# Norm scans and attention angles in the attention's two PSUM banks, with all operations in a new order

## The chip, the cores and the metric

One core of one Trainium2 chip runs the kernel. The time is the device time of one execution in microseconds (us); lower is better. Six engines matter: TensorE (PE, with its weight loads as PEld), VectorE (DVE), ScalarE (ACT), GpSimd (POOL), and SyncE (SP), which issues most DMAs.

## The reference

An attention with a decaying complex state is followed, per token, by a feed-forward network (FFN) with a rational activation. Four batches, eight heads, 768 steps, head width 48; the FFN is 384 to 2048 to 384.

```python
mag = sqrt(a_re**2 + a_im**2)
scale = minimum(mag, 0.999) / (mag + 1e-6)
a_re_n, a_im_n = a_re * scale, a_im * scale
for t in range(S):
    ar, ai = a_re_n[:, :, t, :, None], a_im_n[:, :, t, :, None]
    new_re = ar * S_re - ai * S_im
    new_im = ar * S_im + ai * S_re
    S_re, S_im = new_re + outer(k[t], v[t]), new_im
    y[t] = q[t] @ S_re
x = y.transpose(0, 2, 1, 3).reshape(B * S, H * D)
h = x @ w_in
P = a[0] + a[1]*h + a[2]*h**2 + a[3]*h**3
Q = 1.0 + abs(b[0])*abs(h) + abs(b[1])*h**2
out = (P / (Q + 1e-6)) @ w_out
```

## The kernel before

The 768 steps are cut into 6 chunks of 128; a chunk of one batch is a *unit*, so there are 24 units, taken in 12 pairs. For a unit the decay is turned into magnitude and angle from the chunk's start, so that a chunk becomes ordinary attention plus a carried state.

- `norm` (L498) squares a_re and a_im, gets magnitudes, and runs three scans of 128 columns (L524) that multiply the magnitudes up along the chunk. The second factor of the scans, 1 - 2 EPS x, is written to SBUF over `SQ` (L518) by ACT, DVE or POOL.
- `angle` (L528) works on a pair: ACT's Arctan over `T` (768 columns, L557), one scan over the 768 columns that sums the angles (L539), a maximum for a range test (L540), whole turns as integers in `CO` (the `turn`, L543), their subtraction (L545), and the carry `thc`. Two sines follow (`trig`, L550).
- `outer` (L569) multiplies q and k (`QK`) with magnitudes (`RU`) and then with cosines and sines (`Q`, two halves), and sends them with six DMAs a unit to one of two tiles `HQ`, where heads lie side by side.
- `attn` (L597) does the matmuls of a unit: transposes (L611), evacuated to `kT`; scores (L624), masked to `ST`; values (L642), copied to `X`; state update (L662), added to `St`. Each of these takes one of two PSUM banks (`at`, L337), in turn, in the order in which the code creates them.
- `ffn` (L678) works through the 16 blocks of 128 hidden columns: matmuls into `ph` (L701), eight elementwise instructions on ACT and DVE (one of them, the low product `g`, on POOL or DVE), matmuls into `po` (L717). The first two pairs use full-width float32 weights, later pairs weights split in a high and a low part (`halve`, L461).
- `weights` (L454) reads the weights, which are double precision, in 28 loads and folds them into float32 on ACT, DVE and POOL. `rouse` (L665) adds dummy matmuls in the start.

No engine order follows from the code's order: every operation goes into a `Plan`, and a table (`ORDER`) read by `recorded` gives the order in which operations are issued, and for those that may run on several engines also the engine. Each engine runs its own instructions in that order, and waits by semaphores. In the plan, an operation that uses a PSUM operand is not counted on the port that DVE and POOL share (`port=not psum`, L360).

Of the kernel before, what the change touches and what calls it, by code (L numbers as in the profile page):

```python
# [227 lines left out]
def act(n, psum=False):  # L228
# [11 lines left out]
    "xW?Gfe`CcMEjQAOwT#bRyO5qm=!=T3l;6riEXS*%A9dsSPxdfcOJnmdn<BT#T1GXd{uPU(nzWQAW`R|*2Kn+cZVw%d`8@f*R}toCvcz<<%aoxFrX5werA11z"  # L240
    "a+ND)<d;fF_Tz@obU!1PvFFMuGLLa9kW~U)iVv4bXrNAH)^dsWD%Td>AY+M(kuFW{#SU8VE1ikgR!YKhJ~N|O$;J3oJ}cxkMh~;oq?sJTbg4>P5xEa_B#mP)"
    "W=`OKUzJDdzkO^y{=-;&jhjux%!rP|Khag5lnQ!30l+^PgZZ>IMF#3AwuV}v+v(}iJ@~hza`jT&i%qCWixrrGF?{w@J>?d<4X7>;nPk_CvEE5P71viBUxq@Q"
    "B=QREYVNgjPVVur6zY*KUC!V|J(u@abg3OhYgKqfI3txPPsFn~YRZhjQW=I~sr18H+%5;{`)XN@okZIh943-?Vt2ijQ6<Y|U;G0`Wil<L%AXjuKiSJzB6HA7"
    "R%s>Axl6?A2l0<(0%J3Umg5+UjrF7Gd~9R=?Xh;pmmp;Nx<Z^lk}Q-usz-dfjKWm$e$7QZ=TK1-&iV!qU@t4TuXyw%nRB)Y>trhZtiW@)L-OQhaD07LG#2~x"
    "9yb>QWU<aGt|P<a*U4GpZzSIXh4ghCF2Km7`h$;UnlWw^Hpo%j!1Z3xvt2&o7%b1o3VM@euA<l`oBDFh4#pw_46x)2`Ku|lRRlUks>svK@OnHg)0wxK(x2bI"
    ")s5Xl^nISL=`QFoc9cnxnl4G25KCt{`)}wb#~8!jSjk`C>e+UZ8SD-d0}(09JR>7q8LqNMx9E<}=V3Y8bI0f8CfW@1D(AbuqIZD$mvnaVFjSz22}!!k(GR#C"
    "dLn0ij8t>LUd46NtFlfyasTDmrH{y4tfO&yl6ze<uI>m<lG{$oOI-a5*=`{#IhEP{9=DSHK9ZS?!w51+4Aaa``!MUZg|6c6;h2}@3*2Q6;1TQNdPHt!6clSs"
# [865 lines left out]
```

## Time and profile before

| | |
|---|---|
| median of 3 runs | 608.46 us (607.23 to 609.35) |
| the profiled execution | 608.84 us |
| its span in the trace | 607.1 us |
| TensorE busy | 558.8 us, 92% |
| DVE busy | 545.7 us, 90% |
| ACT busy | 527.1 us, 87% |
| POOL busy | 275.4 us, 45% |

"Busy" is the sum of an engine's instructions; weight loads run beside matmuls and are counted apart. A page of the profile gives these sums, the timeline lists single instructions in order of time with the idle time before them and its releaser in brackets, and the table of stretches gives busy time by engine for parts of the span. `PEclk` is the granted TensorE clock as a share of 2.4 GHz; 0.5 is the lower level, 1.2 GHz.

### The profile page before, as it was taken

Reading aid. Unit: us, or ns where it says so; the run is one execution under the profiler, and the core shown is the slowest. Engines: PE = TensorE matmul, PEld = TensorE weight load, DVE = VectorE, ACT = ScalarE, POOL = GpSimd, SP = SyncE. Lnnn points to the kernel's source line nnn. Section 1 sums busy time; section 2 is a strip of 40 time slices with the busy share of each in tenths; the row PEclk is TensorE's granted clock in tenths of the full one; section 3 lists DMA queues with packets and bytes.
Section 4 is the critical chain, followed back from the end, with each engine's and each line's share of the span. In section 5 each row is a group of like instructions: output and inputs, shape, how many; then the busy total and the mean of one; then the engine's idle time right before and its main releaser. Section 6 shows DMA issues by size and latency. Waiting matters only on the chain.

```text
span 607.1 us, 15647 instructions
## 1 busy us (share of the span) xinstructions
PE 558.8 (92%) x6236; PEld 468.3 (77%) x6236; DVE 545.7 (90%) x918; ACT 527.1 (87%) x870; POOL 275.4 (45%) x264
## 2 busy tenths in 40 slices
PE   3258989999999999998999999999999999999995
PEld 2246878778899999996888877888888888778884
DVE  6989979989999999999999999988899978779983
ACT  6978989989999999999999989988978787587871
POOL 4456455255655556624684544464726066200000
PEclk9669999999999999999999999999999999999998
DMA  8899436436551455537227147233464235010001
GB/s 268 282 253 285 148 79 152 111 57 149 110 136 41 89 128 127 129 103 154 51 64 157 35 106 168 74 60 82 75 102 127 26 73 103 3 52 2 1 1 58
DMA packets 39185, 64.02 MB, mean 105 GB/s; under 512 B 4416, under 2 KB 25152, under 8 KB 39104
## 3 DMA queue, kind: packets, MB, share of 16 engines
q1 hardware_dynamic: 38960, 62.67, 42.2%
q8 instruction: 51, 0.84, 0.6%
q14 instruction: 30, 0.25, 0.1%
q10 hardware_dynamic: 144, 0.26, 0.1%
HBM read 39.32 MB, written 4.72 MB: 73 GB/s over the span
## 4 chain that ended last, share of the span: by engine, by line
PE 47%; DVE 5%; ACT 3%; issue 1%; DMA 1%; DVEq 0%; ACTq 0%
PE po L717 20%; PE ph L701 20%; PE at L642 3%; PE at L624 2%; ACT Zf L366 1%; DVE Af L351 1%; PE at L662 1%; DVE Q L351 1%; DVE ph L351 1%; DMA AA<-in_aa 1%; PE at L611 1%; ACT Af L366 1%; DVE ST L351 0%; DVE g L351 0%; DVE MM L351 0%
## 5 line engine op out<-in xcount | busy, mean ns | idle before, releaser
L717 PE MATMUL po<-g,wh 128*128 128x512 f32 (+1 forms) x576 | 167.6, 360 | 0.0
L701 PE MATMUL ph<-X,wiH 128*128 128x512 f32 (+1 forms) x576 | 144.3, 363 | 2.2 <-DVE Af L351 2.2
L717 PE MATMUL po<-g,wo 128*128 128x256 f32 (+1 forms) x462 | 141.8, 370 | 0.1
L717 PEld LDWEIGHTS po<-g,wh 128*128 128x128 f32 x576 | 102.8, 189 | 18.2 <-issue 1.4
L701 PEld LDWEIGHTS ph<-X,wiH 128*128 128x128 f32 x576 | 97.3, 188 | 20.1 <-issue 1.4
L717 PEld LDWEIGHTS po<-g,wo 128*128 128x128 f32 x462 | 87.3, 191 | 12.5 <-DVE g L351 0.5
L351 POOL TENSOR_TENSOR g<-Af,Zf 128x512 fp32r<-128x512 f32 x30 | 40.2, 1341 | 115.7 <-ACT Zf L366 59.9
L351 DVE SCALAR_TENSOR_TENSOR ph<-Zf,co,ph 128x512 f32<-128x512 f32 x96 | 71.8, 748 | 8.9 <-ACT Zf L366 5.9
L366 ACT ACTIVATE Zf<-ph,co 128x512 f32<-128x512 f32 x96 | 65.3, 680 | 10.4 <-PE ph L701 5.6
L351 DVE SCALAR_TENSOR_TENSOR g<-ph,co,Zf 128x512 fp32r<-128x512 f32 x80 | 59.6, 745 | 14.7 <-ACT Zf L366 13.6
L366 ACT ACTIVATE Zf<-Af,co 128x512 f32<-128x512 f32 x80 | 57.8, 723 | 16.3 <-DVE ph L351 13.9
L366 ACT ACTIVATE Af<-Af,co 128x512 f32<-128x512 f32 x96 | 68.7, 720 | 0.8
L701 PE MATMUL ph<-X,wi 128*128 128x512 f32 (+1 forms) x264 | 67.4, 359 | 0.0
L351 DVE SCALAR_TENSOR_TENSOR Af<-Af,co,g 128x512 f32<-128x512 f32 x80 | 65.1, 814 | 2.2
L366 ACT ACTIVATE Af<-ph 128x512 f32<-128x512 f32 x96 | 56.2, 589 | 8.8 <-PE ph L701 8.6
L351 DVE SCALAR_TENSOR_TENSOR Af<-ph,co,Af 128x512 f32<-128x512 f32 x80 | 59.7, 746 | 1.4
L701 PEld LDWEIGHTS ph<-X,wi 128*128 128x128 f32 x264 | 45.7, 188 | 8.1
L366 ACT ACTIVATE Zf<-Zf 128x512 f32<-128x512 f32 x80 | 50.4, 630 | 1.8
L701 PE MATMUL ph<-wh,wi 128*128 128x256 f32 x192 | 45.9, 387 | 0.9 <-DVE g L351 0.9
L701 PEld LDWEIGHTS ph<-wh,wi 128*128 128x128 f32 x192 | 35.6, 190 | 7.1 <-issue 1.6
L351 POOL TENSOR_TENSOR SQ<-SQ 128x384 f32<-128x384 f32 x18 | 21.8, 1212 | 35.9 <-ACT SQ L366 35.8
L624 PEld LDWEIGHTS at<-HQ 96*32 96x32 f32 x1536 | 30.6, 113 | 9.7 <-ACT kT L357 3.7
(203 smaller groups left out, 1088.7 us busy)
## 6 DMA issues: line engine op xcount, KB each, us to landing
HQ<-Q SPq DMA_DIRECT2D x144, 128.0 KB, 5.0
AA<-in_aa SPq DMA_DIRECT2D x23, 384.0 KB, 4.1
QK<-in_qk SPq DMA_DIRECT2D x23, 384.0 KB, 4.2
V<-in_v SPq DMA_DIRECT2D x24, 320.0 KB, 5.3
wh<-in_w_in SPq DMA_DIRECT2D x6, 512.0 KB, 6.2
g<-in_w_out SPq DMA_DIRECT2D x8, 384.0 KB, 5.6
wh<-in_w_out SPq DMA_DIRECT2D x8, 384.0 KB, 6.4
g<-in_w_in SPq DMA_DIRECT2D x6, 512.0 KB, 6.6
```

The source lines that it names most:

```text
L351: call = lambda e: getattr(e, kind)(*map(real, args), **{k: real(x) for k, x in kw.items()})
L366: e.activation(o(), i(), f, **kw)
L611: e.transpose(pt[:, i].bitcast(F32R), hq[:, 4 * g + i, 1, :], ident)
L624: e.matmul(pst[32 * q:32 * q + 32, i + y, s0:C], hf[:, h, 1, s0:s0 + 32], hf[:, h, 0, s0:C], start=True, stop=True)
L642: e.matmul(py[32 * y:32 * y + 32, min(j, 2), :], l, sts[h // 4][:, h % 4, :] if q is None else hf[:, h, 0, :], start=q is None and j == 0, ...
L662: e.matmul(pd[m:m + 32, h], kT[:, h, m:m + 32], V[:, n:n + D], start=True, stop=True)
L701: e.matmul(o, wt[f // 4 * NJ + j][:, f % 4 * P:f % 4 * P + P], moving(j, hl), start=n == 0, stop=n == len(prods) - 1)
L717: e.matmul(o[:, cols], wt[:, j * P:j * P + P], gg, start=(f == 0 and n == 0 and cols.start == 0), stop=(f == NFF - 1 and n == len(prods) - ...
```

## The change

It does five things.

1. The factor of the norm scans (`near`) is now written by ACT alone, into one of the two attention banks, and the scans read it there.
2. Arctan writes into both banks, one unit of the pair in each (`u.arc`). Scan, turn, subtraction and maximum run per unit on 384 columns with the bank as source; the subtraction writes the wrapped angle to `T`. The maximum follows the subtraction instead of preceding the turn, and ends the bank's use. The banks are cleared at the start.
3. The bank is no longer given by turns: a second table, `BANKS`, gives the sequence in which uses follow each other, and each use takes the bank that came free longer ago (`share`).
4. Small pieces: the coefficient ratios and checks are cut in two so that POOL may do a part; the last accumulators are evacuated in one piece each instead of two halves by ACT and DVE; sines and Arctan of neighbouring pairs are no longer asked for together.
5. The table `ORDER` is a new one: order and engine of all operations change. `WHOLE_OUT` equals `WHOLE`, so that the places that now use `last` or `split(i, o)` compute what they did.

```diff
+    def share(self):
+        shared = self.rings["at"]
+        code = array.array("H", zlib.decompress(base64.b85decode(BANKS)) if BANKS else b"")
+        self.banks = code if sorted(code) == list(range(len(shared))) else range(len(shared))
+        last = [(-2, None), (-1, None)]
+        for n, k in enumerate(self.banks):
+            b = shared[k]
+            b.bank = i = min((0, 1), key=lambda i: last[i][0])
+            if last[i][1]:
+                for o in b.ops:
+                    o.preds.update(last[i][1].ops)
+            last[i] = n, b
...
+    for x in banks:
+        nc.vector.memset(x, 0.0)
...
-        b = buf(ps, [P, 512], F32, "at", 2)
+        b = buf(ps, [P, 512], F32, "at", 1 << 20)
...
-    plan.op(dict(DVE=(2000, ratios)), ("ab",), ("co",), port=True)
+    plan.op(dict(DVE=(270, inverses)), ("ab",), (("co", 0),), port=True)
+    plan.op(dict(DVE=(1730, ratios), POOL=(3050, ratios)), ("ab", ("co", 0)), ("co",), port=True)
...
-        line(EN["s1"], W, lambda: SQ[:, 1], lambda: SQ[:, 1], -2.0 * EPS, 1.0, (s1,), (s1,))
+        near = at(NJ, C)
+        scal(AF.Copy, W, lambda: near.t, lambda: SQ[:, 1], (s1,), (near,), scale=-2.0 * EPS, bias=1.0)
...
-            vec("tensor_tensor_scan", P, lambda j=j: MM[:, j], lambda j=j: MM[:, j], lambda j=j: SQ[:, 1, j],
-                ncar[:, bb, j:j + 1], ALU.mult, ALU.mult, r=(s1, ("ncar", bb)), w=((MM, j),), more=193)
+            vec("tensor_tensor_scan", P, lambda j=j: MM[:, j], lambda j=j: MM[:, j], lambda j=j: near[:, j],
+                ncar[:, bb, j:j + 1], ALU.mult, ALU.mult, r=(near, ("ncar", bb)), w=((MM, j),), more=193, psum=True)
...
-        vec("tensor_tensor_scan", N, fl_t, flat(smask), fl_t, 0.0, ALU.mult, ALU.add, r=(T,), w=(T,), more=800)
-        vec("tensor_reduce", 96, fl[:, 2, n:n + 2], lambda: T.t.rearrange("p x j (n s) -> p x (j n) s", s=8)[:, :, :, 7], AX.X,
-            ALU.max, apply_absolute_value=True, r=(T,), w=(("fl", 2, n),), more=70)
...
+        for x, arc in enumerate(u.arc):
...
+            vec("tensor_tensor_scan", W, A, flat(smask)[:, 0:W], A, 0.0, ALU.mult, ALU.add, r=(arc,), w=(arc,), more=400, psum=True)
+            turns = lambda x=x, f=flat_: f(CO).bitcast(mybir.dt.int32)
+            vec("tensor_scalar", W, turns, A, 1.0 / (2 * math.pi), None, ALU.mult, r=(arc,), w=((CO, x),), psum=True,
+                eng=EN["turn"], scale=(turns, A, 1.0 / (2 * math.pi), 0.0))
+            vec("scalar_tensor_tensor", W, lambda f=flat_: f(T), turns, -2 * math.pi, A, ALU.mult, ALU.add, r=(arc, (CO, x)), w=((T, x),), psum=True)
+            vec("tensor_reduce", 48, fl[:, 2, n + x:n + x + 1], lambda arc=arc: arc.t.rearrange("p (n s) -> p n s", s=8)[:, :, 7], AX.X,
+                ALU.max, apply_absolute_value=True, r=(), w=(arc, ("fl", 2, n + x)), more=40, psum=True)
...
-            table(AF.Arctan, lambda u=U[x]: u.T.t, U[x].T)
+            U[x].arc = at(W), at(W)
+            for y, b in enumerate(U[x].arc):
+                table(AF.Arctan, lambda b=b: b.t, lambda u=U[x], y=y: u.T[:, y].rearrange("p j t -> p (j t)"), (U[x].T, y), (b,), W)
...
-            for h in range(2) if end else (0,):
-                m = n // (2 if end else 1)
-                cols = slice(h * m, h * m + m)
-                evac(m, lambda ob=ob, cols=cols: ob[:, cols], lambda o=o, cols=cols: o[:, cols], (o, "co"), ((ob, h),),
-                     minus if whole else sc, ("ACT", "DVE")[h:h + 1] if end else None)
+            evac(n, lambda ob=ob, n=n: ob[:, 0:n], lambda o=o, n=n: o[:, 0:n], (o, "co"), (ob,), minus if last else sc)
...
-        if i:
-            trig(pairs[i + 1], pairs[i + 2])
-        else:
-            trig(pairs[1], [])
+        trig(pairs[i + 1], [])
         back(i + 1)
-        if not i:
-            trig([], pairs[2])
+        trig([], pairs[i + 2])
```

What the new order makes of this is shown at three places. The first is POOL in the start, where the first pair's Q are made (`QK` and the first `Q` rows belong to unit 0, the `wh` rows to unit 1, whose QK, RU and Z borrow weight tiles). Before:

```order
L351 COPY thc<-T 128x6
L351 TENSOR_TENSOR QK<-QK,RU 128x768
L351 TENSOR_TENSOR Q<-QK,T 128x768
L351 TENSOR_SCALAR MM<-SQ 128x384
L351 TENSOR_TENSOR T<-AA,SQ 128x384
L351 TENSOR_TENSOR wo-1_286<-MM,wo-1_286 128x384
L351 TENSOR_TENSOR wh_284<-MM,wh_284 128x3x128
L351 TENSOR_TENSOR Q<-wh_230,T 128x768
L351 COPY ncar<-MM 128x3
L351 TENSOR_TENSOR Q<-wh_230,CO 128x768
L351 COPY ncar<-MM 128x3 x2
```

Now:

```order
L373 TENSOR_TENSOR RU<-MM,RU 128x3x128
L373 TENSOR_TENSOR QK<-QK,RU 128x768
L373 TENSOR_TENSOR SQ<-SQ 128x384
L373 COPY thc<-T 128x6
L373 TENSOR_SCALAR MM<-SQ 128x384
L373 TENSOR_TENSOR Q<-QK,T 128x768
L373 TENSOR_TENSOR wo-1_243<-MM,wo-1_243 128x384
L373 TENSOR_TENSOR wh_215<-wh_215,wh_241 128x768
L373 TENSOR_TENSOR Q<-wh_215,T 128x768
L373 TENSOR_TENSOR SQ<-SQ 128x384
L373 TENSOR_SCALAR MM<-SQ 128x384
L373 TENSOR_TENSOR Q<-wh_215,CO 128x768
```

Unit 1's product QK (`wh_215<-wh_215,wh_241`) has come to POOL from DVE, and its two Q products stand closer behind it.

The second place is ACT at about the same time, around the first evacuation of transposes (`kT`). Before:

```order
L439 ACTIVATE g<-g 128x512
L431 ACTIVATE ph<-g 128x384
L439 ACTIVATE g<-g 128x384
L357 ACTIVATE kT<-at_112 128x384
L439 ACTIVATE g<-g 128x384
L357 ACTIVATE kT<-at_111 128x384
L366 ACTIVATE SQ<-AA 128x768
L431 ACTIVATE po_418<-g 128x512
L465 ACTIVATE wiH_429<-wi_236 128x512
L366 ACTIVATE RU<-MM 128x3x128
L431 ACTIVATE ph<-wh_384 128x512
L439 ACTIVATE wh_384<-wh_384 128x512
```

Now:

```order
L464 ACTIVATE g<-g 128x512
L367 DMA HQ_95<-Q 16x8x256
L388 ACTIVATE SQ<-AA 128x768
L456 ACTIVATE ph<-g 128x384
L456 ACTIVATE po_316<-wh_313 128x384
L367 DMA HQ_96<-Q 16x8x256
L464 ACTIVATE wh_313<-wh_313 128x384
L464 ACTIVATE g<-g 128x384
L388 ACTIVATE SQ,fl<-SQ 128x768
L456 ACTIVATE ph<-g 128x384
L464 ACTIVATE g<-g 128x384
L367 DMA HQ_96<-Q 16x8x256
```

Three of the rows of now are DMA issues to the two `HQ` tiles (two more follow a few rows later); before, SP issued all of these.

The third place is TensorE in the middle of the program, where a unit's scores (32 partitions, shapes 32x96 to 32x32) are followed by state update (L662 before, L693 now) and values (32x128). Before:

```order
L624 MATMUL at_112<-HQ_96 32x32 x2
L717 MATMUL po_2806<-g,wh_1101 128x256
L717 MATMUL po_2806<-g,wo_1669 128x256
L717 MATMUL po_2806<-g,wh_1101 128x256 x2
L717 MATMUL po_2806<-g,wo_1669 128x256
L717 MATMUL po_2806<-g,wh_1101 128x256
L717 MATMUL po_2813<-g,wh_1101 128x256
L717 MATMUL po_2813<-g,wo_1669 128x256
L717 MATMUL po_2813<-g,wh_1101 128x256
L662 MATMUL at_111<-V,kT 32x48 x24
L642 MATMUL at_112<-ST,V 32x128 x16
L642 MATMUL at_112<-HQ_96,St 32x128 x16
```

Now:

```order
L655 MATMUL at_111<-HQ_96 32x96 x2
L655 MATMUL at_111<-HQ_96 32x128 x2
L655 MATMUL at_111<-HQ_96 32x64 x2
L655 MATMUL at_111<-HQ_96 32x32 x2
L693 MATMUL at_112<-V,kT 32x48 x24
L673 MATMUL at_111<-ST,V 32x128 x16
L673 MATMUL at_111<-HQ_96,St 32x128 x16
L748 MATMUL po_3667<-g,wh_1817 128x512
```

The FFN matmuls (`po`) that stood between scores and state update have moved behind the values.

## Rows read from the trace of the kernel before

**Rows 1.** The page's first part: busy us, share of the span, instructions.

```profile
PE 558.8 (92%) x6236; PEld 468.3 (77%) x6236; DVE 545.7 (90%) x918; ACT 527.1 (87%) x870; POOL 275.4 (45%) x264
```

**Rows 2.** Table of stretches: length, busy by engine (instructions), granted clock, DMA share, GB/s.

```profile
0.00:15.00 15.00, 4.64 (x11) 3.77 (x12) 10.09 (x35) 9.54 (x18) 6.16 (x20) 1.00 0.80 268
15.00:30.00 15.00, 4.24 (x11) 2.97 (x11) 14.20 (x25) 14.37 (x24) 6.95 (x7) 0.63 0.86 285
30.00:45.00 15.00, 8.73 (x101) 6.60 (x102) 11.99 (x25) 11.37 (x23) 7.39 (x10) 0.61 1.04 252
45.00:60.00 15.00, 12.60 (x207) 9.98 (x201) 13.59 (x26) 12.94 (x27) 9.20 (x12) 0.96 0.94 292
...
90.00:105.00 15.00, 14.85 (x192) 12.10 (x191) 14.59 (x30) 13.94 (x24) 8.75 (x12) 0.89 0.57 133
...
250.00:300.00 50.00, 47.83 (x743) 41.63 (x743) 48.33 (x82) 46.52 (x77) 23.85 (x21) 1.00 0.46 101
```

**Rows 3.** Timeline of TensorE in the start: start, length, engine, line, operation, idle before.

```profile
50.41 0.86 PE L611 MATMUL at<-ident,HQ 128*128 128x128 f32 x8 [1.92 <-DMA HQ<-Q]
...
55.42 2.86 PE L701 MATMUL ph<-wh,wi 128*128 128x256 f32 x12
```

**Rows 4.** Timelines of ACT, POOL and SP in the start.

```profile
58.63 0.58 ACT L366 ACTIVATE Af<-ph 128x512 f32<-128x512 f32 x1
...
24.54 1.82 POOL L351 TENSOR_TENSOR Q<-QK,T 128x768 f32<-128x768 f32 x1 [0.26 <-ACT T L565]
...
35.30 1.80 POOL L351 TENSOR_TENSOR Q<-wh,T 128x768 f32<-128x768 f32 x1 [1.19 <-DVE wh L351]
...
41.49 1.84 POOL L351 TENSOR_TENSOR Q<-wh,CO 128x768 f32<-128x768 f32 x1
...
40.09 5.12 SPq L345 DMA_DIRECT2D HQ<-Q  x6
```

**Rows 5.** TensorE's waits from 62 to 600 us: total us, times, longest.

```profile
PE at L611 <- DMA HQ<-Q: 2.8, 2, 2.0
PE ph L701 <- DVE Af L351: 2.2, 5, 0.7
PE at L611 <- DVE QK L351: 1.6, 1, 1.6
PE at L624 <- ACT kT L357: 1.2, 2, 1.0
...
PE at L642 <- DVE ST L351: 0.9, 3, 0.4
```

**Rows 6.** Instructions by tile or line: count, then ns minimum/median/maximum, first and last start.

```profile
L351 DVE TENSOR_TENSOR_SCAN MM<-MM,ncar,SQ x69: 450/475/1230, 12.2 to 492.7; 128x128 f32<-128x128 f32 x69
L351 DVE TENSOR_TENSOR_SCAN T<-smask,T x12: 1730/1744/1907, 17.8 to 451.1; 128x768 f32<-128x768 bf16 x12
L351 DVE TENSOR_TENSOR ST<-at,cmask x48: 672/682/692, 43.6 to 522.2; 128x512 f32<-128x512 f32 x48
L351 DVE TENSOR_TENSOR g<-Af,Zf x50: 657/692/1181, 176.0 to 596.7; 128x512 fp32r<-128x512 f32 x50
L351 POOL TENSOR_TENSOR g<-Af,Zf x30: 1277/1297/1844, 194.2 to 593.7; 128x512 fp32r<-128x512 f32 x30
L351 DVE TENSOR_TENSOR QK<-QK,RU x11: 942/948/958, 67.0 to 489.0; 128x768 f32<-128x768 f32 x11
L351 POOL TENSOR_TENSOR QK<-QK,RU x12: 1804/1855/2415, 22.5 to 503.4; 128x768 f32<-128x768 f32 x12
```

**Rows 7.** Groups by line: busy us, mean ns of one, idle before.

```profile
L366 ACT ACT_TABLE_LOAD x23 | 29.5, 1283 | 0.9 <-DVE ph L351 0.5
```

**Rows 8.** Timeline of the end: last evacuation in two halves, and its output DMA.

```profile
600.08 0.47 ACT L357 ACTIVATE wo<-po,co 128x256 f32<-128x256 f32 x1 [0.82 <-PE po L717]
...
600.59 0.48 DVE L351 TENSOR_SCALAR wo<-po,co 128x256 f32<-128x256 f32 x1 [0.81 <-ACT wo L357]
...
601.11 0.38 ACTq L345 DMA_DIRECT2D out<-wo  x1
```

More of the change, by code (lines that the diff above doesn't have):

```diff
@@ L44 @@
 HQB, QB, VB = 2, 2, 2
-WHOLE = 2
+WHOLE, WHOLE_OUT = 2, 2
 VP = 64
@@ L240 @@
[L240 to L247, printed above, removed]
@@ L564, in run @@
             trigs.append(f)
-            e.activation(x(), x(), f, **kw)
-        plan.op(dict(ACT=(act(2 * W), run)), (key,), (key,)).tab = 1
+            e.activation(o(), x(), f, **kw)
+        plan.op(dict(ACT=(act(n), run)), (key,), to or (key,)).tab = 1
     def outer(c, bb):
@@ L675, in rouse, with ffn @@
                 n += 1
-    def ffn(c, xs, b0, whole=False, end=False):
+    def ffn(c, xs, b0, whole=False, last=False, end=False):
         T = 2 * C * len(xs)
@@ L686, in ffn @@
         keys = [(x, b) for x, _ in xs for b in range(2)]
-        ns = 1310 if whole else 9 * (MM512 if F == 1 else 123)
+        ns, ns2 = (1310 if x else 9 * (MM512 if F == 1 else 123) for x in (whole, last))
         pend = []
@@ L705, in reduce @@
                 f = F * k + x
-                r = (wo[f],) if whole else ((wh[f // 3], f % 3), woL[f])
+                r = (wo[f],) if last else ((wh[f // 3], f % 3), woL[f])
                 def run(e, f=f, x=x):
-                    if whole:
+                    if last:
                         prods = ((wo[f], g[:, x * T:x * T + T]),)
@@ L731, in ffn @@
             b_ = buf(ff, [P, 512], F32, "Zf", ZB)
-            z_ = buf(ps, [P, 512], F32, "po2") if whole else b_
+            z_ = buf(ps, [P, 512], F32, "po2") if last else b_
             ta, tb, tz, tp = ((lambda y=y: y.t) for y in (a_, b_, z_, ph))
@@ L740, in ffn @@
             scal(ROOT, 512, tz, ta, (a_, "co"), (z_,), bias=ks, more=93)
-            scal(AF.Square, 512, tz, tz, (z_,), (z_,), psum=whole)
-            if whole:
+            scal(AF.Square, 512, tz, tz, (z_,), (z_,), psum=last)
+            if last:
                 g = buf(ff, [P, 512], F32, "g", GB)
@@ L974, in checks @@
         scal(AF.Abs, 4, lambda: cf[:, 0:4], lambda: av, ("ab",), ("cf",))
[L975 to L976 removed]
+        plan.op(dict(DVE=(1500, coefs_ok), POOL=(2100, coefs_ok)), ("ab", "cf"), ("cf",), port=True)
+        plan.op(dict(DVE=(700, coefs_sum)), ("cf",), (("cnt", 1),), port=True)
+        plan.op(dict(DVE=(930, values_ok)), (*(("fl", i, n) for i in range(2) for n in range(NC * B)), *(("fl", 2, n) for n in range(NC * B)),
                                             *(("ncar", b) for b in range(B))), (("cnt", 0), "fl"), port=True)
@@ L1012, in attn_moe @@
     mark = len(plan.ops)
+    each(norm, 1)
+    plan.spread(mark, -0.3, 0.2)
+    mark = len(plan.ops)
     back(0)
@@ L1016, in attn_moe @@
     mark = len(plan.ops)
-    each(norm, 1)
     trig([], pairs[1])
@@ L1044, in attn_moe @@
         plan.spread(mark, i - (0 if i < 2 * WIDE else 1), i + 1)
-        if i == WHOLE - 1:
-            mark = len(plan.ops)
-            split()
-            plan.spread(mark, WHOLE - 0.7, WHOLE + 0.5)
+        for x in sorted({WHOLE, WHOLE_OUT}):
+            if i == x - 1:
+                mark = len(plan.ops)
+                split(x == WHOLE, x == WHOLE_OUT)
+                plan.spread(mark, x - 0.7, x + 0.5)
     plan.close()
```

143 lines of the change are left out of this document (79 added, 64 removed).

## The prediction

> **What bounds the kernel now.** I read the page's first part, then the table of stretches, then what TensorE waits for. TensorE is busy 558.8 of 607.1 us [rows 1], and the change adds no real matmul to it (one dummy of `rouse` more), so the time moves only with TensorE's 48.3 idle us. The stretches say where these lie: 10.4 + 10.8 + 6.3 + 2.4 = 29.8 us before 60 us [rows 2]; about 7 us after its last matmul [rows 8]; the rest, some 11 us, is strewn over the 520 us between. In that middle DVE and ACT are nearly as full as TensorE: from 250 to 300 us the three are busy 47.8, 48.3 and 46.5 of 50 [rows 2]. The reader is to see two places where time can be had: the start, where the first FFN matmul comes at 55.4 us [rows 3], and a middle that three engines bound together.
>
> The start is a chain. Two units must pass norm, angles, sines and the products Q, be redistributed by six DMAs each (HQ), be transposed and scored before the first FFN matmul. Unit 1's transposes run at 50.41 us, and the FFN starts 5.0 us after them [rows 3]. Unit 1 is late because of its Q: GpSimd makes the sine half at 35.30, the cosine half only at 41.49 us, and SyncE issues all six HQ DMAs from 40.09 to 45.21 us; the transposes follow 5.2 us after that [rows 4].
>
> **The change, part by part.**
>
> *Start.* In the new order GpSimd makes unit 1's product QK and both halves of Q almost back to back (one 384-wide sum and its clip between), and five of the twelve HQ DMAs stand on ACT's queue, where they no longer wait behind SyncE's weight loads. I walk the new GpSimd rows with the durations of the trace. The pair's angle chain ends about where it did (the coefficient ratios leave DVE's head, but the two scans wait for unit 1's T, which GpSimd now makes). Unit 0's sine product starts at 24.5 us now and takes 1.8 [rows 4]; behind it come one 384-wide product on GpSimd (half of 1.86 by width) and two on DVE with their hand-overs, so unit 1's QK can start at about 29. It takes 1.86 us [rows 6], the sine half 1.8, sum and clip about 1.5, the cosine half 1.84 [rows 4]: the latter ends near 37 instead of 43.3 us. The last HQ DMAs, behind some short ACT work, go out near 40 instead of 45.2, so unit 1's transposes come near 45.5 and the FFN near 50: about 5 us earlier. ACT bounds this: its first FFN instruction stands at 58.63 us [rows 4], behind about the same work as now (five fold steps and six halvings go from before it; one table load, half-width angle pieces and the five DMA issues come in), and it idles 15 x 4 - (9.5 + 14.4 + 11.4 + 12.9) = 11.8 us in the first 60 [rows 2]. If half of that idle time goes, ACT allows 5 to 6 us; if none, about 1. I take **-4.2 us**, bounds 0 and -7.
>
> *What moves between engines.* GpSimd takes 13 more of the FFN's low products g (0.69 us each on DVE, 1.30 on GpSimd), eight more 768-wide products (0.95 on DVE, 1.86 on GpSimd) [rows 6] and some twenty narrower ones of about half the width. DVE loses 9.0 + 7.6 + about 11 = 28 us. It gains 14 turn steps that were ACT's (nearest row: a 512-wide PSUM operand at 0.68 us [rows 6], by width about 0.55: +7.7), four evacuations (+2.7), small copies (+2), and what splitting costs. For that, a scan of 128 takes 0.475 and one of 768 takes 1.744 [rows 6], so 1.98 ns an element; 384 is 0.98, and 24 of these for 12 of 768 are +2.7; the split steps behind them and the maxima about +5. DVE: -8 us net. ACT loses six table loads of 1.28 us [rows 7] and some weight halvings, and gains the copies for the norm scans that were GpSimd's and the second half of each Arctan: net some -8, bounds 0 and -16. GpSimd rises by about 50 from 275 us [rows 1], and stays the least loaded of the four.
>
> *PSUM operands.* On DVE 158 instructions now read PSUM that read SBUF before: 72 norm scans, 24 angle scans, and the turns (14), subtractions (24) and maxima (24) behind them. No scan of the trace reads PSUM. The nearest rows are a 512-wide product with a PSUM source, 0.682 us, and one with both sources in SBUF, 0.692 us [rows 6]: no surcharge. I take 0, bounds -10 and +65 ns each. The Trainium skill, Perfetto Trace Analysis, section Optimizing Scalar/DVE Operations, puts DVE's access overhead at about 60 ns on SBUF and 125 ns on PSUM; by that, as an estimate from the page, 158 instructions would cost DVE 10.3 us more, against this change.
>
> *The shared port.* Some DVE instructions with two SBUF operands take far longer than their median: the norm scans have median 0.475 and maximum 1.230 us, the products g 0.692 and 1.181 (on GpSimd 1.297 and 1.844) [rows 6]. So DVE and GpSimd hold each other up. The change takes 72 x 0.475 + 12 x 1.744 = 55 us of scans out of that, and hands GpSimd 50 us. The Trainium skill, SBUF — State Buffer, section SBUF: two separate sides, says that a DVE instruction with two SBUF inputs and a GpSimd one that reads SBUF exclude each other for a whole instruction; the long maxima agree with it.
>
> *Middle.* Relief: from 62 us on TensorE's listed waits are for HQ (2.8), for DVE in the FFN (2.2), for a product QK (1.6) and for the transposes' evacuation (1.2 in two) [rows 5]. With DVE and ACT 8 us lighter each and the port freer I take **-5** of about 11, bounds 0 and -9. Against it stands the new order of TensorE: attention steps stand in blocks. Transposes are followed at once by scores at 7 places (2 before), and the values have at most 1.0 us of other work behind the last scores at 9 (4 before). The first kind waits 0.6 us each (1.2 in two), the second 0.3 (0.9 in three) [rows 5]: 5 x 0.6 + 5 x 0.3 = **+4.5**, bounds 0 and +9. What is queued behind such a wait is the next FFN block; it costs in full, as nothing overtakes on TensorE. Moving the maximum behind the turn takes one short step out of the angle chain, which FFN matmuls hide: 0.
>
> *End.* The last accumulator is now evacuated whole by ACT instead of in halves by ACT and DVE. But the halves ran one behind the other: ACT 600.08, DVE 600.59 to 601.07, output DMA issued at 601.11 [rows 8]. A whole one on ACT, about 0.62 us by twice the half's width, allows the DMA at about 600.75: **-0.4**. The rest (ratios and checks in pieces, two clears of the banks at the start, under 2 us in all on engines that idle there) I cost at nothing; the start's idle time covers it.
>
> *Sum.* The profiled execution took 608.84 us, 0.4 above the median. 608.84 - 4.2 - 5.0 + 4.5 - 0.4 = 603.7; less 0.4 for the median, rounded to half a us: **603.5**.
>
> **The rivals.**
>
> *Slower: the banks.* Attention, norm copies and angles share two banks, and a pair's angles take both from Arctan until the maximum, which now ends their use. In the second pair of the new order 29 DVE rows lie between the first angle scan and the last maximum. If DVE or GpSimd runs late there, the next unit's transposes wait for a bank, and with them all of TensorE. Today's waits for HQ are 1.4 us in the mean [rows 5]. If each of ten pairs costs 1.2 us in that way, the 12 us give 615.5. It ends on the slower side from 0.7 us a pair (5 of gain and 1.8 of margin over ten). For it: GpSimd gets 50 us more, and its products already run up to a third over their median (2.415 against 1.855) [rows 6]. Against it: the new TensorE order has long FFN stretches without attention (one of 198 FFN matmuls), which leave room for the angles.
>
> *No change: the start is not TensorE's to win.* ACT is 0.96 busy from 15 to 30 us [rows 2]. If its folds and the DMA traffic hold the first FFN instruction, the start gives 1 us, and the middle -0.5: 607.
>
> *No change: PSUM operands cost.* With +65 ns on 158 instructions (the upper bound above) DVE is no lighter, the relief of 5 us is gone, and the time is 608.5. The rule cited above is this case; the rows speak against it.
>
> *Faster by more.* The start gives 6 and the blocks cost nothing: 597.
>
> **How the numbers follow.** Forecast 603.5: 0.45. Faster by more, 597: 0.15. Start not won, 607: 0.13. PSUM costs, 608.5: 0.07. Banks, 615.5: 0.20. About 0.3% (1.8 us) is what a measurement of this kernel can tell from no change. Faster by more than that: 0.60; within it: 0.20; slower: 0.20. The range is 596 to 611.5: below, a start of -7 with the middle's relief and few block waits; above, no gain at the start and block waits at twice their price. It leaves out most of the banks' case.
>
> **What would show it.** Right: the first FFN matmul near 50 us and the first transposes of unit 1 near 45.5; TensorE's idle time after 62 us still about 11 us, now before scores and values; DVE and GpSimd busy near 538 and 325 us; PSUM scans at 0.45 to 0.50 us (128) and near 1.0 (384), without the long maxima; no more than 44 table loads. Wrong: unit 1's transposes still near 50 us (start); waits before the transposes themselves of 1 us and more in most pairs, or a granted clock under 1.0 in a stretch after 110 us, as now from 90 to 105 us (0.89, behind TensorE idling) [rows 2] (banks); norm scans at 0.54 or more (PSUM).

## The result: slower, 616.9 us, and where TensorE idles now

The changed kernel takes 616.93 us (median of 4 runs, 612.95 to 617.46), the kernel before 608.9 beside it: ratio of the means 1.0119, 95% interval 1.0070 to 1.0169. The forecast was 603.5 with a range of 596 to 611.5; both the sign and the range were missed. The profiled execution took 617.46 us, its span is 615.7.

First the totals of the profile after (the page's first part), which answer to [rows 1]:

```profile
PE 557.7 (91%) x6238; PEld 469.9 (76%) x6238; DVE 541.8 (88%) x948; ACT 513.7 (83%) x866; POOL 310.8 (50%) x306
```

DVE got 3.9 us lighter, ACT 13.4, GpSimd 35.4 heavier, TensorE does the same. So no engine has more to do than before except the least loaded one, and the time still rose by 8.6 us of span. TensorE's idle time rose by 9.8 (58.0 against 48.3). Where, says the table of stretches (length, then busy us of PE, PEld, DVE, ACT, POOL with instructions, granted clock, DMA share, GB/s), first of before, then of after:

```profile
0.00:30.00 30.00, 8.88 (x21) 6.75 (x22) 24.30 (x59) 23.91 (x42) 13.11 (x27) 0.81 0.83 276
30.00:62.00 32.00, 23.33 (x351) 18.14 (x349) 27.50 (x54) 26.24 (x52) 18.49 (x24) 0.80 0.98 271
62.00:120.00 58.00, 54.30 (x470) 45.13 (x462) 53.88 (x92) 54.31 (x90) 26.79 (x36) 0.97 0.45 113
120.00:590.00 470.00, 462.26 (x5366) 390.32 (x5366) 432.29 (x704) 418.16 (x682) 215.68 (x178) 1.00 0.38 84
```

```profile
0.00:30.00 30.00, 10.31 (x24) 7.49 (x24) 27.34 (x57) 24.73 (x46) 21.83 (x33) 1.00 0.87 294
30.00:62.00 32.00, 19.81 (x331) 15.64 (x332) 18.47 (x39) 17.07 (x35) 12.38 (x28) 0.73 0.92 235
62.00:120.00 58.00, 58.00 (x536) 49.97 (x535) 55.65 (x105) 55.39 (x96) 37.60 (x42) 1.00 0.43 119
120.00:590.00 470.00, 450.68 (x5270) 381.73 (x5269) 425.15 (x728) 404.52 (x673) 237.71 (x205) 1.00 0.37 85
```

Read length minus PE's busy time. Up to 120 us TensorE idles 33.5 us before and 31.9 after, a gain of 1.6 where 4.2 were forecast for the start. From 120 to 590 us it idles 7.7 before and 19.3 after: 11.6 us lost where the forecast had a net gain of 0.5. The row 30 to 62 shows that the start did not go as planned either: DVE, ACT and GpSimd all work less there (18.5, 17.1 and 12.4 us against 27.5, 26.2 and 18.5). Something stops everyone.

*The start.* GpSimd ended where it was forecast: unit 1's product came at 26.62 us, its sine half at 28.78, its cosine half was done at 35.9 instead of 43.3 ([rows 4]). From its timeline:

```profile
21.07 2.11 POOL L373 TENSOR_TENSOR Q<-QK,T 128x768 f32<-128x768 f32 x1 [0.38 <-ACT T L596]
...
32.51 0.99 POOL L373 TENSOR_TENSOR SQ<-SQ 128x384 f32<-128x384 f32 x1 [1.91 <-ACT SQ L388]
...
34.06 1.82 POOL L373 TENSOR_TENSOR Q<-wh,CO 128x768 f32<-128x768 f32 x1
```

The transposes came later all the same (timelines of TensorE and ACT in the start; rows of before: [rows 3]):

```profile
52.50 0.72 PE L642 MATMUL at<-ident,HQ 128*128 128x128 f32 x4 [3.76 <-DMA HQ<-Q]
...
60.13 1.56 PE L732 MATMUL ph<-wh,wi 128*128 128x256 f32 x6
...
41.02 3.58 ACTq L367 DMA_DIRECT2D HQ<-Q  x2
44.66 0.63 ACT L456 ACTIVATE po<-g 128x512 f32<-128x512 f32 x1 [5.54 <-DMA HQ<-Q]
```

52.50 instead of 50.41 (forecast 45.5), and the first FFN matmul at 60.13 instead of 55.42 (forecast 50). The last two rows give the place: an HQ DMA in ACT's instruction stream has to wait, ACT stands still for 5.54 us, and the fold work queued behind it with it. The chain of waits shows three HQ transfers one behind the other (start, length):

```profile
27.65 9.27 DMA HQ<-Q
36.94 7.10 DMA HQ<-Q
44.06 8.30 DMA HQ<-Q
```

The second and the third go out at the moment at which the one before has landed (27.65 + 9.27 = 36.92; 36.94 + 7.10 = 44.04), although the last product had been done at 35.9. So what held them was an earlier transfer and not their data. Why one waits for the other, the trace does not say.

In the kernel before, on SyncE, the row of six DMAs in [rows 4] is two batches. Three stood behind weight loads until 40.09 us; the last three go out as the cosine half ends (41.49 + 1.84 = 43.33) and wait for nothing else:

```profile
43.36 1.85 SPq L345 DMA_DIRECT2D HQ<-Q  x3
```

*The middle.* TensorE's waits from 62 to 600 us, which answer to [rows 5] (total us, times, longest):

```profile
PE ph L732 <- DVE Af L373: 12.1, 11, 2.2
PE at L655 <- ACT Af L388: 1.1, 1, 1.1
```

The waits for HQ and for a product QK are gone, that of the scores for the transposes' evacuation is down from 1.2 to 0.5 us. In their place TensorE waits for DVE in the FFN: a block needs a PSUM buffer ph that DVE has not yet read out. The waits of DVE and ACT from 120 to 590 us, before and after; the first two rows of each are waits for TensorE inside the attention, the last two ACT's waits inside the FFN:

```profile
DVE ST L351 <- PE at L624: 1.5, 3, 0.9
...
ACT X L366 <- PE at L642: 6.3, 7, 1.9
...
ACT Zf L366 <- DVE ph L351: 12.9, 23, 1.9
...
ACT Zf L366 <- POOL g L351: 1.2, 3, 0.8
```

```profile
DVE ST L373 <- PE at L655: 8.7, 11, 1.4
...
ACT X L388 <- PE at L673: 11.9, 12, 4.0
...
ACT Zf L388 <- DVE ph L373: 22.0, 31, 2.2
...
ACT Zf L388 <- POOL g L373: 6.9, 8, 2.2
```

In the new order the attention of a pair of units stands closer together on TensorE: from the second pair on, the values of its two units begin 7 to 14 us apart, in the median 9.7 (before 8 to 38, median 14.2). During it DVE and ACT wait 7.2 and 5.6 us more than before. The five longest of TensorE's waits for Af come 12 to 20 us behind its last attention matmul, where it runs the FFN alone. ACT's waits inside the FFN grew by a little more: 9.1 us for DVE's use of ph, and 5.7 us for the low product g on GpSimd, which now makes 43 of these instead of 30 (1.30 us each, on DVE 0.69). So the place of the attention is one candidate for the loss in the middle, and the longer low product is another.

*PSUM operands, table loads, end.* The scans by tile (ns minimum/median/maximum; [rows 6] before), the table loads ([rows 7]) and the last evacuation with its DMA ([rows 8]):

```profile
L373 DVE TENSOR_TENSOR_SCAN MM<-MM,ncar,at x72: 447/469/482, 8.6 to 499.0; 128x128 f32<-128x128 f32 x72
...
L373 DVE TENSOR_TENSOR_SCAN at<-smask,at x24: 933/961/962, 15.0 to 505.3; 128x384 f32<-128x384 bf16 x24
```

```profile
L388 ACT ACT_TABLE_LOAD x20 | 25.7, 1283 | 0.8 <-DVE ph L373 0.5
L594 ACT ACT_TABLE_LOAD x13 | 16.7, 1283 | 0.2
L596 ACT ACT_TABLE_LOAD x7 | 9.0, 1283 | 0.2
```

```profile
608.89 0.69 ACT L379 ACTIVATE wo<-po,co 128x512 f32<-128x512 f32 x1
609.61 0.39 ACTq L367 DMA_DIRECT2D out<-wo  x1
```

Scans on PSUM take what they took on SBUF, and their long maxima (1230 ns) are gone; six table loads are gone (40 in the rows above; 46 before, of which [rows 7] shows 23); the last output DMA goes out 0.75 us behind the last matmul's end (608.86) instead of 1.07.

The collisions of DVE with GpSimd did not leave the FFN. Its step Af, with two operands in SBUF, before and after:

```profile
L351 DVE SCALAR_TENSOR_TENSOR Af<-Af,co,g x80: 722/751/2349, 173.6 to 595.1; 128x512 f32<-128x512 f32 x80
```

```profile
L373 DVE SCALAR_TENSOR_TENSOR Af<-Af,co,g x80: 731/752/2454, 168.6 to 603.7; 128x512 f32<-128x512 f32 x80
```

Each of those over 0.9 us (8 before, 11 after) lies beside a GpSimd instruction. In sum the 80 take 65.1 us before and 68.5 after, and 65.7 in the run e1 below, where the middle still loses 8.6 us: these collisions are not what the middle lost there.

### The profile page after: what moved, and what is told of

The parts are those of the page before. It is cut to its first block, busy times and chain, and to the rows that moved or that the text cites. A ratio compares the mean times of both kernels' runs of the same rounds, so it can differ in the third digit from the quotient of the medians.

```text
span 615.7 us, 15767 instructions
## 1 busy us (share of the span) xinstructions
PE 557.7 (91%) x6238; PEld 469.9 (76%) x6238; DVE 541.8 (88%) x948; ACT 513.7 (83%) x866; POOL 310.8 (50%) x306
## 4 chain that ended last, share of the span: by engine, by line
PE 57%; ACT 16%; DVE 14%; DMA 7%; issue 4%; POOL 1%; SPq 0%; DVEq 0%; ACTq 0%; POOLq 0%
PE po L748 22%; PE ph L732 22%; PE at L673 5%; ACT Zf L388 5%; DVE Af L373 4%; DMA HQ<-Q 4%; PE at L655 3%; DMA QK<-in_qk 3%; ACT Af L388 3%; DVE g L373 2%; DVE ph L373 2%; PE at L693 2%; PE at L642 2%; DVE ST L373 1%; ACT L594 1%
## 5 line engine op out<-in xcount | busy, mean ns | idle before, releaser
L748 PE MATMUL po<-g,wh 128*128 128x512 f32 (+1 forms) x576 | 165.7, 359 | 0.9 <-DVE g L373 0.9
L732 PE MATMUL ph<-X,wiH 128*128 128x512 f32 (+1 forms) x576 | 143.9, 364 | 12.2 <-DVE Af L373 12.1
L748 PE MATMUL po<-g,wo 128*128 128x256 f32 (+1 forms) x462 | 139.7, 366 | 0.0
L373 POOL TENSOR_TENSOR g<-Af,Zf 128x512 fp32r<-128x512 f32 x43 | 56.4, 1316 | 114.2 <-ACT Zf L388 53.5
L748 PEld LDWEIGHTS po<-g,wo 128*128 128x128 f32 x462 | 87.0, 189 | 12.1 <-issue 0.2
L373 DVE SCALAR_TENSOR_TENSOR Af<-Af,co,g 128x512 f32<-128x512 f32 x80 | 68.5, 858 | 2.4
L373 POOL TENSOR_TENSOR Q<-QK,T 128x768 f32<-128x768 f32 x17 | 34.3, 2018 | 33.8 <-ACT T L596 24.3
L373 DVE TENSOR_TENSOR ST<-at,cmask 128x512 f32<-128x512 f32 x48 | 31.4, 685 | 14.8 <-PE at L655 14.6
```

What stands on the lines that cost most here:

```text
L373: call = lambda e: getattr(e, kind)(*map(real, args), **{k: real(x) for k, x in kw.items()})
L732: e.matmul(o, wt[f // 4 * NJ + j][:, f % 4 * P:f % 4 * P + P], moving(j, hl), start=n == 0, stop=n == len(prods) - 1)
L748: e.matmul(o[:, cols], wt[:, j * P:j * P + P], gg, start=(f == 0 and n == 0 and cols.start == 0), stop=(f == NFF - 1 and n == len(prods) - ...
```

## The experiments

Theory for the start: the five HQ DMAs on ACT's queue hold ACT. Rival: the transfers are slow, whoever issues them. Theory for the middle: it is the order, rival: it is the two banks and their operands. (The runs do not separate these two cleanly.) All times are medians; the kernel before took 608.0 to 608.9 beside each group of runs.

### The start: who issues five DMAs

The changed kernel with all HQ DMAs on SyncE (e1):

```diff
             o.eng = list(o.ways)[x // 4096]
+            if o.eng == "ACT" and "SP" in o.ways and o.tail > 5000:
+                o.eng = "SP"
```

> The changed kernel with one thing undone: the five HQ DMAs of the first two units that stood on ACT's queue are issued by SyncE, in the same place of the order; everything else keeps its place. Theory 'the DMAs block ACT' (ACT issues in order, and an HQ DMA that has to wait holds all ACT work behind it): ACT's gaps from 28 to 45 us go, unit 1's transposes come at 47 to 49 us instead of 52.5, the first FFN matmul at 54 to 56 us instead of 60.1, time 611 to 613 us. Rival 'the transfers themselves are slow' (DMA traffic, whoever issues them): unit 1's transposes stay at 51 to 53 us, the FFN at 59 to 61, time 616 to 618 us. The waits for Af in the middle (12 us after 110 us) stay in both.

611.2 us (ratio to before 1.0052, 1.0030 to 1.0075): 5.7 us come back by the medians. (By the means it is 4.5: the four runs of the changed kernel lie between 612.95 and 617.46, the twelve of e1 between 609.01 and 613.43.) TensorE's rows of the start, and its largest wait:

```profile
47.57 0.53 PE L644 MATMUL at<-ident,HQ 128*128 128x128 f32 x4 [0.58 <-ACT wh L381]
...
56.69 1.56 PE L734 MATMUL ph<-wh,wi 128*128 128x256 f32 x6
```

```profile
PE ph L734 <- DVE Af L375: 9.0, 8, 2.2
```

The transposes are 4.9 us earlier and no longer wait for HQ; the first FFN matmul, at 56.7 us, is 0.7 later than the theory had it. Up to 120 us TensorE now idles 27.8 us (before 33.5), so the start gives 5.7: more than the forecast's 4.2, once the DMAs are away from ACT. From 120 to 590 us 16.3 us of idle time stay, 3.0 fewer than with the DMAs on ACT, and the waits for Af, which I had expected to stay at 12, fell to 9.0: part of the price of the five DMAs is paid far behind them.

The converse, the kernel before with the same five DMAs on ACT (e4):

```diff
             o.eng = list(o.ways)[x // 4096]
+            if x % 4096 in (191, 209, 206, 204, 205):
+                o.eng = "ACT"
```

> The kernel before with one thing added: five HQ DMAs of the first two units (one of unit 0, four of unit 1) are issued by ACT instead of SyncE, the same five as in the changed kernel, at their places in the old order. Theory 'the DMAs block ACT': ACT shows gaps of 1 to 5 us before the work behind them between 26 and 50 us, unit 1's transposes and the first FFN matmul come 2 to 5 us later (FFN at 57 to 60 us instead of 55.4), time 610 to 614 us. Rival 'the transfers themselves': no change, 607 to 610 us.

616.8 us (1.0156, 1.0109 to 1.0203), 8.0 more than before, and outside even the theory's range:

```profile
58.74 1.23 PE L613 MATMUL at<-ident,HQ 128*128 128x128 f32 x8 [9.60 <-DMA HQ<-Q]
...
50.70 0.56 ACTq L347 DMA_DIRECT2D HQ<-Q  x1
```

The expected gaps on ACT did not show. Here it goes the other way round: the DMA stands behind ACT's arithmetic and goes out at 50.7 us, where SyncE had issued the last one by 45.2 [rows 4]; then it lands late too (the transposes follow 8.0 us after the issue, before 5.2). In both kernels it is one coupling: ACT issues in order, so a DMA waits for ACT's work and ACT's work for the DMA. The Trainium skill, DMA: Bandwidth & Descriptors, section Issuing engines are not separate DMA queues, says that issuing from several engines saves only the sequencer's time of issue, as all run on the same 16 DMA engines. Both runs agree that nothing is won, and add a price of 5.7 and 8.0 us.

Unit 1's attention in one compact piece on TensorE (e8b; e8 is the same with another table of banks):

```diff
-T(first half) S S T(second half) V D FFN FFN
+T(first half) T(second half) S S V FFN FFN D
```

> The changed kernel with the HQ DMAs on SyncE (611.2 us), and unit 1's attention in one compact piece on TensorE: second transposes right behind the first, scores, values, then the first two FFN blocks, the state product behind them (in the run before, it took 9.1 us from the first transposes at 47.6 to the FFN at 56.7, against 5.0 us in the kernel before). Theory 'the start is lost on TensorE between transposes and FFN': first FFN matmul at 52 to 54.5 us, time 607 to 609.5 us. Rival 'ACT holds the start': the first FFN matmul comes earlier, ACT's first FFN instruction stays at 59 to 60 us, time 610.5 to 612.5 us.

> As the run with unit 1's attention compact (625.1 us), but with the changed kernel's own table of banks, only unit 1's six uses re-dealt among themselves. Theory 'the start is lost on TensorE between transposes and FFN': first FFN matmul at 52 to 54.5 us, time 607 to 609.5 us. Rival 'ACT and DVE hold the start' (the last run showed the first FFN matmul at 56.4 in spite of the new order): the FFN stays at 55.5 to 57 us, time 610 to 612.5 us.

e8 took 625.1 us, and its loss grew in steps far behind unit 1; I put that down to its bank table, which led to e9 below. e8b took 612.4: the first FFN matmul came at 53.8, as the theory had it, and nothing was won by it. The 1.7 us lead of unit 1's values over e1 was 0.4 by unit 17, and the last unit's came 1.3 us behind e1's. In this order an earlier first FFN matmul is not worth its length.

### The middle: banks, operands, order

The changed kernel in its own order, with the angles in SBUF (e2):

```diff
-            A = lambda arc=arc: arc.t
+            A = lambda x=x: T[:, x].rearrange("p j t -> p (j t)")
...
-            vec("tensor_tensor_scan", W, A, flat(smask)[:, 0:W], A, 0.0, ALU.mult, ALU.add, r=(arc,), w=(arc,), more=400, psum=True)
+            vec("tensor_tensor_scan", W, A, flat(smask)[:, 0:W], A, 0.0, ALU.mult, ALU.add, r=((T, x),), w=((T, x),), more=400, psum=True)
```

> The changed kernel in its own order, instruction for instruction, but the angles stay in SBUF: Arctan, scans, turns and subtractions work in place on T, so that no angle holds one of the two PSUM banks and 62 DVE instructions read SBUF instead of PSUM. The maxima read a constant of the same shape, so the guard on the angles' range is left out. Theory 'the order' (what costs in the middle is where the new order puts the steps, not the banks): within 2 us of the changed kernel, 615 to 619 us, and the waits of TensorE for Af in the FFN stay at 9 to 14 us. Rival 'the banks' (angles hold banks, PSUM operands cost): 605 to 611 us, with the waits after 110 us down to the 8 us of the kernel before.

639.3 us (1.0501, 1.0464 to 1.0538): neither. Rows of DVE by tile, beside 961 ns at most 962 for the scan above:

```profile
L373 DVE TENSOR_TENSOR_SCAN T<-smask,T x24: 941/1188/2012, 15.8 to 525.5; 128x384 f32<-128x384 bf16 x24
...
L373 DVE TENSOR_TENSOR T<-T,thc x20: 133/706/1744, 112.6 to 524.4; 128x3 f32<-128x3 f32 x20
```

Even an add of three elements has a median of 706 ns. By the timelines the slow ones lie beside a GpSimd product: the scan at 196.92 us took 1.71 us beside one that began at 196.79, the scan at 245.51 us took 0.96 with none beside it. The add just before the latter took 1.74 us and ended at 245.47, as a GpSimd product begun at 242.95 ended (245.46):

```profile
242.95 2.51 POOL L373 TENSOR_TENSOR QK<-QK,RU 128x768 f32<-128x768 f32 x1
243.73 1.74 DVE L373 TENSOR_TENSOR T<-T,thc 128x3 f32<-128x3 f32 x1
```

The Trainium skill, SBUF — State Buffer, section SBUF: two separate sides (the exclusive lock cited in the prediction), says that of a DVE instruction with two SBUF inputs and a GpSimd one that reads SBUF the later is blocked until the earlier has ended; this add agrees.

DVE is busy 24.4 us longer (566.2), and the time is 22.4 us up. So in this order, with GpSimd's extra 35 us beside the angles, PSUM operands are worth 22 us, net of what it may help that the angles no longer hold the banks. They gain nothing over the kernel before, whose order kept those scans clear (1730 to 1907 ns, [rows 6]).

The changed instructions in the old order: first with banks by first use (e3, 776.1 us), then with each use waiting for a free bank (e3b); and the same with only the norm copies in the banks (e5 683.2, e5b):

```diff
-            b.bank = i = min((0, 1), key=lambda i: last[i][0])
+            b, i = shared[k // 2], k % 2
```

> The changed kernel's instructions (norm scans and angles in PSUM, maximum behind the subtraction) in the order of the kernel before: each step that both have stands where it stood before, on the engine it had, the halves side by side, HQ DMAs on SyncE; the seven norm copies that were GpSimd's are ACT's. Banks in order of first use. Theory 'the order': near the kernel before, 606 to 612 us, the first FFN matmul at 54 to 57 us, TensorE's listed waits for Af after 62 us under 5 us. Rival 'the banks': 614 to 622 us, with waits before transposes and scores of 1 us and more in most pairs.

> As the run of the changed instructions in the old order (776 us), with the banks dealt out with care: a use takes a bank only once the one before it there is through, and what finds none free is put off until one is (96 puttings-off, 25 places on ACT and on DVE where the old sequence is broken, 17 on TensorE). Theory 'norm scans and angles in the two banks cannot be had in the old order' (an angle pair holds both banks over a chain on ACT and DVE, and attention has to wait): over 630 us. Rival 'the 776 us were a bad dealing of banks': 608 to 625 us.

> As the run of the old order with the banks shared (776 us), but only the norm copies and scans are in the banks; the angles are in SBUF and in place, the maxima read a constant (the guard on the angles' range is left out). Theory 'it is the angles that the old order cannot take' (an angle holds a bank over a chain of steps on two engines, a norm copy over three scans): 608 to 618 us. Rival 'any sharing of the two banks breaks the old order': over 640 us.

> As the run of the old order with the banks dealt out with care (766 us), but only the norm copies and scans use the banks; the angles are in SBUF, in place and in halves, the maxima read a constant (the guard on the angles' range is left out). Theory 'it is mostly the angles that hold the banks too long': 610 to 640 us. Rival 'the norm copies do as much': over 660 us (the same kernel with the banks dealt out by first use took 683).

e3b: 766.0 us (1.2596, 1.2563 to 1.2630); e5b: 674.1 (1.1063, 1.1016 to 1.1110). TensorE's waits in e3b, then in e5b:

```profile
PE ph L732 <- DVE Af L373: 14.8, 8, 5.4
PE at L693 <- ACT CO L379: 14.0, 1, 14.0
PE at L673 <- DVE fl L373: 11.6, 1, 11.6
...
PE at L642 <- DVE fl L373: 10.1, 2, 5.5
```

```profile
PE at L655 <- DVE ST L373: 15.5, 10, 6.1
...
PE at L673 <- DVE MM L373: 3.7, 3, 1.6
```

In e3b the mechanism of the prediction's rival "banks" stands in the rows: state products, values and transposes wait for a turn (CO) or a maximum (fl) that holds the bank. With the norm copies alone in the banks (e5b, angles in SBUF in halves) the time is still some 65 us up; my expectation that it would mostly be the angles missed. Its largest wait names no norm copy, though; the waits for the norm scans (MM) are smaller. Nor is all of it waiting. Between its waits TensorE ran at a lower granted clock; the stretch from 120 to 590 us in e3b:

```profile
120.00:590.00 470.00, 368.06 (x4366) 312.55 (x4366) 327.12 (x560) 337.01 (x552) 169.73 (x153) 0.87 0.31 72
```

The clock is 0.87 there and 0.97 in e5b (before 1.00), and TensorE's busy time over the whole program rose from 558.8 to 606.9 and 578.8 us for the same matmuls. So in the old order, with the banks dealt out in these two ways, neither use can be had. Whether some other order could carry them for less is not shown.

The bank table (e9): the DMAs on SyncE as in e1, and the table that hands out the banks sorted by each use's first instruction. 96 of 181 uses change bank. The steps keep their places on GpSimd and SyncE and shift by a few at 2 spots on TensorE, 11 on DVE and 28 on ACT, where a bank now comes free later. The beginning of the unpacked table, as use numbers in the order in which they get a bank (along it the two banks take turns):

```diff
-BANKS: 1 0 3 2 9 4 8 6 7 5 11 10 15 12 13 14
+BANKS: 0 1 2 3 4 6 9 5 8 7 10 11 12 15 14 13
```

> The changed kernel with the HQ DMAs on SyncE (611.2 us) and nothing else but the table that deals out the two PSUM banks: each use gets the bank in the order of its first instruction, so 96 of 181 uses sit in the other bank; the steps keep their places on GpSimd and SyncE, and shift by a few places at 2 spots on TensorE, 11 on DVE, 28 on ACT, where the bank now frees later. Theory 'the two banks are the tight resource' (the loss of the last run with unit 1 compact came from its bank table, dealt out in this way, and grew in steps through the middle): 618 to 626 us, unit 1's values within 1 us of the run with the DMAs on SyncE, the last unit's values 8 to 14 us later. Rival 'the loss came from unit 1's new place': 610 to 613 us.

621.0 us, 9.7 more than e1, in steps through the middle (unit 1's values 2.2 us earlier than in e1, the last unit's 8.2 later):

```profile
PE ph L732 <- DVE Af L373: 14.5, 10, 4.1
```

Same arithmetic, other banks and the shifts that they ask for: again the wait that grows is the FFN's for Af, not one that names a bank.

The attention pulled apart within its banks (e10): 16 values one or two FFN blocks later, 22 products ST two FFN steps later.

```diff
-TensorE: S S V FFN     DVE: ST ST ffn ffn
+TensorE: S S FFN V     DVE: ffn ffn ST ST
```

> The changed kernel with the HQ DMAs on SyncE (611.2 us), its own table of banks, and the attention behind unit 2 pulled apart a little: on TensorE 16 of the values with fewer than two FFN blocks behind their last scores are moved behind one or two more, and on DVE 22 of the products ST are moved behind the next two FFN steps. Theory 'the blocks of attention cost in the middle' (DVE waits for scores, 14.6 us, and then lacks the time for the FFN): DVE's waits at ST fall below 6 us, TensorE's for Af from 9.0 below 6, time 606 to 609.5 us. Rival 'the banks rule the middle' (what holds a bank longer delays the next use): 611 to 618 us.

643.0 us (1.0583). DVE's waits at ST did fall, to 4.4 us. But ACT, which evacuates the values, stood still instead:

```profile
ACT X L388 <- PE at L673: 44.1, 18, 7.5
```

What I had expected to relieve the blocks made 32 us more. I read it so: what stays longer in a bank, or waits longer at the head of ACT, moves everything behind it. The run does not separate the two.

Four attempts on single engines, each on top of e1, with only the engine or place of the named steps changed:

```diff
 e7_turn_act:  14 turns            -DVE +ACT
 e12_turn_dve: the other 10 turns  -ACT +DVE
 e7_nomax:     24 maxima           -DVE
 e11_fill:     11 ready DVE steps  +ahead of a waiting ST
```

> The changed kernel with the HQ DMAs on SyncE (611.2 us), and in addition the 14 turn steps that the change gave to DVE back on ACT, at the same places of the order: DVE loses 14 x 0.55 = 7.5 us, ACT gains about 6.5. Theory 'DVE is overfull where the FFN runs alone' (the two banks press the attention into runs, so DVE waits for TensorE there, and between them angle steps come on top of the FFN's): TensorE's waits for Af after 62 us fall from 9.0 to 5 us or less, time 606 to 609.5 us. Rival 'it is TensorE's blocks themselves': the waits stay within 2 us of 9.0 and the time within 1.5 us of 611.2; if ACT has no room either, it goes to 612 to 615.

> The changed kernel with the HQ DMAs on SyncE (611.2 us), and the ten turn steps that are still ACT's given to DVE, at the same places: ACT loses about 4.7 us, DVE gains 5.5. Theory 'ACT is late in the angle chain and so holds the banks' (14 turns more on ACT cost 6.7 us): 607 to 610 us. Rival 'DVE is the tighter of the two': 612 to 617 us, waits for Af above 9 us.

> The changed kernel with the HQ DMAs on SyncE (611.2 us), and the 24 maxima of the angles left out (the guard on their range is not computed; its cells are set to zero): DVE loses 24 x 0.196 = 4.7 us, and the banks come free one short step earlier. Theory 'DVE is overfull where the FFN runs alone': waits for Af from 9.0 to 5 to 7 us, time 608 to 610 us. Rival 'TensorE's blocks themselves': waits and time unchanged within 1.5 us.

> The changed kernel with the HQ DMAs on SyncE (611.2 us), and on DVE alone eleven steps that are ready in time (fold, norm and FFN steps, 0.07 to 0.75 us each, five of them behind 120 us) pulled ahead of a product ST at which DVE waited for scores; no other engine's order changes. Theory 'DVE loses its time waiting for TensorE's scores in the blocks' (8.6 us in eleven waits from 120 to 590 us): about 2.5 us of these waits are filled, waits for Af fall by 1.5 to 2.5 us, time 608 to 610 us. Rival 'those waits are not what TensorE later lacks': 610.5 to 613 us.

617.9 (more than either side had expected), 614.7, 610.3 and 611.8 us, beside e1's 611.2. Waits of e12 and of e7_nomax on TensorE, and of e11 on DVE:

```profile
PE ph L732 <- DVE Af L373: 9.8, 8, 2.1
```

```profile
PE ph L734 <- DVE Af L376: 9.0, 7, 2.3
```

```profile
DVE ST L373 <- PE at L655: 6.7, 9, 1.4
```

Turns cost on either engine where they are added. Leaving out the maxima, 4.7 us of instructions, changed TensorE's waits for Af by nothing. But DVE's busy time fell by 1.4 us only (537.9 against 539.3), so this is a test of a small relief; and the 0.9 us between the medians is not clear of the noise (ratio to before 1.0037, 1.0015 to 1.0059; e1 1.0030 to 1.0075). Filling 1.9 of DVE's 8.6 us of waiting for scores gave nothing. None of the four theories of a single full engine was borne out. No run gave the 13 low products back to DVE, so the rival that they slow the FFN stands untested.

## Why the prediction was wrong, step by step

Two steps failed. The larger one is the middle: relief and blocks together were forecast at -0.5 us, and TensorE's idle time there rose by 11.6. The other is the start.

- **Start, -4.2 us: the failed clause is that on ACT's queue the five DMAs "no longer wait behind SyncE's weight loads".** They wait on ACT's queue as well, and hold it. Until 120 us the gain was 1.6 instead of 4.2; with the DMAs on SyncE it is 5.7, and the time 5.7 us better. There was also less to win than the clause says, as the last three of unit 1's DMAs had stood behind no weight load before (row at 43.36 us above). The walk along GpSimd's rows came out (35.9 us against "near 37"), in part by luck: it began 3.4 us earlier than I took (21.07 against 24.5) and lost time to waits that I had left out, 1.9 us of it for ACT's squares.
- **Relief in the middle, -5.0: did not come.** DVE and ACT did get lighter (DVE -3.9 against a forecast -8, ACT -13.4 against -8, GpSimd +35 against +50). The waits that were to shrink were replaced by others, 12.1 us for Af instead of 2.2. In the new order a little less work on DVE (1.4 us of busy time without the maxima) moved none of them; a larger relief was not tried.
- **Attention blocks, +4.5: right direction, wrong place and size.** I looked for waits before scores and values, by [rows 5]. Those are about 2.4 us in all. I had priced TensorE's own waits alone. What grew is the waiting of DVE and ACT during a block, ACT's inside the FFN, and TensorE's for Af behind it. Relief and blocks together were forecast at -0.5; TensorE's idle time from 120 to 590 us rose by 11.6 (8.6 with the DMAs on SyncE).
- **PSUM operands, 0: right.** 469 against 475 ns, 961 against an estimate of 980. The case of +65 ns each, which the prediction took from the Trainium skill, Perfetto Trace Analysis, section Optimizing Scalar/DVE Operations, did not occur. That in this order the time would be 22 us longer without them I had not seen.
- **Table loads, end:** six fewer, and 0.3 instead of 0.4 us.
- **The rival "banks" (615.5 us, 0.20)** came nearest in time, and its mechanism exists: e3b shows it in the rows. In the changed kernel it does not show in the form I gave it (transposes waiting 1.2 us a pair; they wait under 2 us in all). That it came nearest is luck in part: 5.7 of the 8.0 us are the five DMAs, which this rival does not contain. That the new order avoids such waits by its runs of attention, and that the price so moves into the FFN, is my reading and not shown.

Put together: of the 8.0 us by which the change is slower, undoing the five DMAs gives back 5.7. What remains, 2.4 us by the medians (e1 against before, 1.0030 to 1.0075, which is 1.8 to 4.6 us), is what the rest of the change costs: it gains 5.7 us of TensorE's idle time in the start and loses 8.6 in the middle. The cause of the loss in the middle stays open. For the sharing of the banks speaks that neither use of them went into the old order as tried, and that another bank table, with the shifts it asks for, costs 9.7 us. Not tried are the new order without any sharing, free of the collisions of e2, and the new order with the 13 low products on DVE. Six attempts to take the loss away (e7 twice, e8b, e10, e11, e12) did not. No version run here beats the kernel before.

## What to carry to other kernels

- A DMA on a computing engine's queue is an instruction in that engine's order. Before moving one there, ask what it waits for, what stands behind it, and what it stands behind.
- Sharing a buffer can take orders away. Ask of a shared bank not whether its users fit by their lengths, but which order of the engines it still allows, and who idles in that order.
- Relief of a busy engine is worth something only where the wait that ends last is for that engine's load. Take some of its work away in a run before booking it as a gain, and read from the profile how much busy time really went.
